# Attention with a threshold, then a Fourier mix and a two-layer network: row statistics behind the masking, a new order of early transfers and a fifth room for raw weights

## The chip, the core and the metric

The kernel runs on one core of one Trainium2 chip. The time is the device time of one execution in microseconds (us). The kernel before takes 1598.78 us, the median of three runs (1594.14 to 1601.38).

## What is computed

The inputs are q, k and v (8 batches, 8 heads, 576 rows, 64 columns, FP32), a scalar tau and two weight matrices that come in 64 bits (512 x 2048 and 2048 x 512).

```python
scores = q @ k.T / 8
scores = where(scores >= max(scores) - tau, scores, -1e9)      # per row
attn = softmax(scores);  x = attn @ v                          # heads side by side: 576 x 512
u = x + real(fft(fft(x, rows), columns))
un = (u - mean(u)) / sqrt(var(u) + 1e-6)                       # per row of 512
out = u + relu(un @ w_ch1) @ w_ch2
```

## The kernel before, in words

**Steps.** A batch has four pairs of heads, a pair five tiles of 128 query rows, so a batch is 20 steps and the kernel 160. A step computes scores of a tile for both heads (L434; L440 for the last, half tile), row maxima on VectorE (L455, in late steps L512), exponentials on ScalarE (L463, L518), and on VectorE the masking, which compares scores with the threshold, multiplies and sums (L471, L532). The scores stand in two PSUM tiles of two banks each, so the next step's scores wait for the masking. The tile of the step before is transposed on TensorE (L579 to L597) and copied to SBUF by ScalarE; at tiles 1 and 3 a product with v follows (L628).

**Everything is in an order written out by hand.** Each engine takes its instructions in program order, and so does SyncE, whose queue holds nearly all transfers. A transfer is asked for where its call stands in the program, and one that must wait for its room holds back all that are behind it.

**The first batch** (`step`) runs attention alone, filled up with small products (`busy`, L111). Beside it the first weight matrix comes in as 16 chunks of 512 KB. `staged` (L323) gives a chunk its room of raw 64-bit numbers in `hs`: four rooms, in turn. `convert` turns a chunk into FP32 in stages, one call of `next` each: the request (L283), two integer operations on VectorE (L293, L296), two on ScalarE (L301, L304), an add on VectorE (L308), a product on GpSimd (L313), a sign on ScalarE and another product on GpSimd (L315, L316). Step i takes the first stage of chunk i between its maxima and its masking, and the add and last stages of chunk i-1; its request for chunk i+3 comes near its end. Column means of the weights (L357) follow at step 6 and on. Ahead of step 0 stand the requests for the first chunks, for the two Fourier tables (`load_dim` L238 and L240, `load_seq` L215 and L217; L240 and L217 overwrite part of what the request before them brought, and wait for it) and for v; GpSimd copies the tables into their places (`copy_dim`, `copy_seq`, which ends by clearing the tile `f`, L228).

**The second batch** (`second_batch`, steps 20 to 39, numbered `first` = 0 to 19) also mixes batch 0 and begins the network on its rows, in portions that `fill` hands out. The 16 chunks of the second matrix are converted beside it. PLAN gives for each chunk the step of its first stage, the chunk, the room of its raw numbers and the step that asks for it: `h0` to `h3` are rooms in `hs`, a digit is a part of the second matrix's own tile that is not yet filled, `tmp` is a scratch tile. `transfers(first)` (L1634) asks for the chunks of a step, behind its masking.

**The late batches** run attention of one batch beside mix and network of the one before. Groups of 512 rows go through the network in a form with fewer products (`two_level`, L1179 and L1366). `Rows.load` (L837 to L847) transposes 128 rows of u, copies them with four ScalarE instructions (L842, L843) and takes their statistics on VectorE at once (L845, L846). A late step hands out network work three times: `fill(True)` between the exponentials and the masking (`softmax_second`), and two more behind it. `Rows.factors` (L852) takes the square root of the four tiles' variances on ScalarE, with two table loads (L853, L856), and a reciprocal on VectorE (L857). At a batch change the folds of the last pair (L679 to L695) and of the whole batch (L710 to L741) run on VectorE, and the first products of the mix (L751) wait for them.

Of the kernel before, what the change touches and what calls it, by code (L numbers as in the profile page):

```python
# [9 lines left out]
FP32 = mybir.dt.float32  # L10
# [37 lines left out]
def kernel(  # L48
# [12 lines left out]
    nc = tc.nc  # L61
# [12 lines left out]
    WC = 512  # L74
# [7 lines left out]
    sb = ctx.enter_context(tc.tile_pool(name="sb", bufs=2))  # L82
# [153 lines left out]
    def load_dim():  # L236
        raw = sb.tile([128, DM], FP32, tag="tmp", bufs=1, name="dim_raw")
        nc.sync.dma_start(out=raw[:, :], in_=dft_dim[0:128, :])  # L238

        nc.sync.dma_start(out=raw[0:1, EH:DM], in_=dft_dim[128:129, EH:DM])  # L240
        return raw
# [79 lines left out]
        return run  # L321

    def staged(n, src, dst):  # L323
        c0 = (0, 3 * WC, 6 * WC, 13 * WC)[n % 4]
        stage = hs[:, c0 : c0 + 3 * WC].bitcast(INT32).rearrange("p (c n) -> p c n", c=3)
        return chunk(src, dst, stage[:, 0:2, :], stage[:, 2, :])

    def w1_chunk(n):
        g, c = divmod(n, ND)
        cols = slice(WC * g, WC * (g + 1))  # L330
        return staged(n, w_ch1[128 * c : 128 * (c + 1), cols], w1[c][:, cols])
# [61 lines left out]
    def scale_q(n):  # L393

        raw = loaded[n][0]
        nc.scalar.activation(out=raw[:, :], in_=raw[:, :], func=ACT.Copy, scale=q_scale[:, :])
# [96 lines left out]
    def spread_inverse(i):  # L493
        e, den = steps[i]
        if i % NT == 4:
            nc.scalar.copy(e[:, S : S + 64], e[:, 512:S])
        if den is None:
            return
        nh = den.shape[1]
        rec = sb.tile([128, 2 * D], FP32, tag="rec", name="rec")  # L500
        nc.scalar.copy(
            rec[:, :].rearrange("p (j d) -> p j d", j=nh), _repeated(den, 2 * D // nh)
        )
        steps[i] = (e, rec)
# [309 lines left out]


    warm = const.tile([128, 1], FP32, name="warm")
    out_rows = out.rearrange("b s d -> (b s) d")

    COLS1, COLS2 = 28 * 4096, 49 * 2048
# [5 lines left out]
    class Rows:  # L825
# [7 lines left out]
        def load(self, t):  # L833
            c0 = (self.first + 128 * t) % RING
            pn = ps.tile([128, 512], FP32, tag="mm", bufs=4, name="pn")
            for c in range(ND):
                nc.tensor.transpose(  # L837
                    pn[:, 128 * c : 128 * (c + 1)], u_t[:, c, c0 : c0 + 128], ident[:, :]
                )
            u = sb.tile([128, DM], FP32, tag="u", bufs=4, name="u")  # L840
            for c in (0, 256):
                nc.scalar.copy(u[:, c : c + 129], pn[:, c : c + 129])  # L842
                nc.scalar.copy(u[:, c + 129 : c + 256], _reversed(pn[:, c + 129 : c + 256]))  # L843
            stats = sb.tile([128, nc.vector.BN_STATS_DIM], FP32, tag="stats", name="stats")
            nc.vector.bn_stats(stats[:, :], u[:, :])  # L845
            nc.vector.bn_aggr(self.mv[:, t, :], stats[:, :])  # L846
            self.us[t] = u  # L847

        def loaded(self):
            return all(u is not None for u in self.us)  # L850

        def factors(self):  # L852
            nc.scalar.activation(  # L853
                out=self.rstd[:, :], in_=self.mv[:, :, 1], func=ACT.Sqrt, bias=eps[:, :], scale=1.0
            )
            nc.scalar.activation(out=warm[:, :], in_=eps[:, :], func=ACT.Exp)  # L856
            nc.vector.reciprocal(self.rstd[:, :], self.rstd[:, :])  # L857
# [584 lines left out]
    late = []  # L1442
    ended = []
# [31 lines left out]
    def step(i):  # L1475

        n, t = divmod(i, NT)
        scores(i)

        def stages(count):  # L1480
            for _ in range(count if i - 1 in chunks else 0):
                next(chunks[i - 1], None)

        def next_stages():
            if i in chunks:
                next(chunks[i])
            stages(2)

        def last_stage():
            stages(1)  # L1490
            chunks.pop(i - 1, None)

        if t == 1 and n > 0:
            softmax(i, lambda: weighted_values(n - 1, 1), next_stages, last_stage)
            load_v(n + 1)
        elif t == 3:
            softmax(i, lambda: weighted_values(n, 0), next_stages, last_stage)
        else:
            softmax(i, None, next_stages, last_stage)
        if t == 1 and n > 0:  # L1500
            pass
        elif later and later[0][0] <= i:
            later.pop(0)[1](i)
        else:
            busy(2 if i < NCHUNK else 1)
        if t == 2:
            scale_q(n + 1)
        if t == 3:
            prep_pair(n + 1)
        if t == 1:  # L1510
            prep_ends(n)
        if i > 0:
            transposed_weights(i - 1)
        if i in chunks:
            next(chunks[i])
        while after and after[0][0] <= i:
            after.pop(0)[1]()
        if i > 0 and i + 3 < NCHUNK:
            chunks[i + 3] = w1_chunk(i + 3)
        if t == 2 and n > 0:  # L1520
            folds.append(fold_rows(n - 1))
        if folds and next(folds[0], True):
            folds.pop(0)
        spread_inverse(i)

    folds = []
    later = []
# [21 lines left out]
        means[g] = mean  # L1549

    chunks = {0: w1_chunk(0)}
    raw = load_dim()
    load_seq()
    chunks[1] = w1_chunk(1)
    scale_q(0)
    prep_pair(0)
    load_v(0)
    chunks[2] = w1_chunk(2)
    chunks[3] = w1_chunk(3)
    load_v(1)  # L1560
    copy_dim(raw)
    copy_seq()
    LAST = HID // WC - 1
    for g in range(LAST):
        center(g)
# [4 lines left out]
    while after:  # L1570
# [1 line left out]

    PLAN = (
        (1, 15, "h0", 0), (2, 14, "h1", 0), (3, 13, "h2", 0), (4, 12, "h3", 0),
        (5, 11, "0", 0), (5, 10, "1", 0), (6, 9, "2", 0), (7, 8, "h3", 5),
        (8, 7, "0", 6), (8, 6, "1", 6), (9, 5, "tmp", 4), (9, 4, "h3", 8),
        (10, 3, "0", 9), (11, 2, "h3", 10), (12, 0, "tmp", 10), (14, 1, "tmp", 13),
    )
    chunks = {}

# [4 lines left out]
    def transfers(first):  # L1585
        for at, j, room, issue in PLAN:
            if issue == first:
                chunks.setdefault(at, []).append(second_chunk(j, room))
# [30 lines left out]
    def second_batch(i):  # L1619

        nonlocal budget
        n, t = divmod(i, NT)
        first = i - per_batch
        if first != 1:
            scores(i)
        if first == 0:

            transposed_weights(i - 1)
        softmax(
            i, None, lambda: (advance(first), advance(first - 1), advance(first - 1)),  # L1630
            lambda: advance(first - 1),
        )
        chunks.pop(first - 1, None)
        transfers(first)  # L1634
        fold_more()
        if first == 0:
            weighted_values(n - 1, 1)
            scores(i + 1)
            column_means(LAST)
            copy_mean(LAST)  # L1640
            folds.append(fold_rows(n - 1))
            while folds:
                fold_more()
            load_v(n + 1)
            start_batch(0)
            mix(3)
            mix(3)
        elif first == 1:
            mix(3)
            transposed_weights(i - 1)  # L1650
            mix(2)
            mirrored(LAST)
            for c, eng in ((1, nc.vector), (3, nc.vector), (0, nc.gpsimd), (2, nc.gpsimd)):
                less_mean(eng, LAST, c)
            advance(first)
        elif first == 2:
            mix(2)
            transposed_weights(i - 1)
            mix(2)
            weighted_values(n, 0)  # L1660
            advance(first)
        else:
            fill()
            transposed_weights(i - 1)
            advance(first)
            fill()
            if t == 3:
                prep_pair(n + 1)
            fill()
            if t == 2:  # L1670
                weighted_values(n, 0)
            if t == 0:
                weighted_values(n - 1, 1)
                folds.append(fold_rows(n - 1))
                load_v(n + 1)
        if t == 1:
            prep_ends(n)
        if t == 2:
            scale_q(n + 1)
        if first == 16:  # L1680
            fold_halves(1)
        if first < 3:
            budget += 3 * per_slot
        spread_inverse(i)
# [8 lines left out]
    for i in range(2 * per_batch, total):  # L1693
# [20 lines left out]
        fill(True)  # L1714
        if i < total:
            softmax_second(i)
        while held:
            held.pop(0)()
        if mixes:
# [62 lines left out]
    for _ in range(3):  # L1782
        mix(1)
        fill(True)
        while held:
            held.pop(0)()
        if wanted:
            wanted.pop().factors()
    ended.append(True)
    per_slot = cost(0) / 40  # L1790
    while mixes or work:
# [47 lines left out]
```

## Time and profile before

| | |
|---|---|
| median of three runs | 1598.78 us |
| the profiled execution | 1596.7 us |
| its span, first to last instruction | 1594.9 us |
| mean granted TensorE clock | 0.990 |
| idle before scores (L434) for the masking (L471), first 330 us | 15.7 us, 11 times |
| idle of VectorE before L293 for a chunk's transfer, first 330 us | 12.3 us, 5 times |
| idle of VectorE before the statistics (L845) | 52.2 us, 28 of 36 times |
| SyncE's queue, waiting in L283 for rooms, first 330 us | 64.3 us |

A window row gives busy time and number of instructions of each engine in that stretch, then the granted TensorE clock (1.00 is full), the share of the transfer engines and the traffic. A timeline row gives start and length in us, the engine, the line, what is written and read, how often, and in brackets how long the engine stood idle before it and what ended that. PE is TensorE, PEld its weight loads, DVE VectorE, ACT ScalarE, POOL GpSimd, SPq SyncE's queue. A matrix product counts twice[...].

### The profile page before, as it was taken

Reading aid. Unit: us, or ns where it says so; the run is one execution under the profiler, and the core shown is the slowest. Engines: PE = TensorE matmul, PEld = TensorE weight load, DVE = VectorE, ACT = ScalarE, POOL = GpSimd, SP = SyncE. Lnnn points to the kernel's source line nnn. Section 1 sums busy time; section 2 is a strip of 40 time slices with the busy share of each in tenths; the row PEclk is TensorE's granted clock in tenths of the full one; section 3 lists DMA queues with packets and bytes.
Section 4 is the critical chain, followed back from the end, with each engine's and each line's share of the span. In section 5 each row is a group of like instructions: output and inputs, shape, how many; then the busy total and the mean of one; then the engine's idle time right before and its main releaser. Section 6 shows DMA issues by size and latency. Waiting matters only on the chain.

```text
span 1594.9 us, 27001 instructions
## 1 busy us (share of the span) xinstructions
PE 1538.0 (96%) x9786; PEld 1189.4 (75%) x9786; DVE 1060.9 (67%) x2119; ACT 918.6 (58%) x1921; POOL 775.2 (49%) x961
## 2 busy tenths in 40 slices
PE   7989989999999999989999999999999999999999
PEld 4555445555888777877787778877787778889999
DVE  6887766755868566775668466756567566655546
ACT  5875766554665666656666567656666676222231
POOL 5672554024445552646253643545264725546735
PEclk9999999999999999999999999999999999999999
DMA  5523221556956354634455344634464434646655
GB/s 149 132 67 115 75 77 37 152 156 206 292 174 198 93 159 128 202 97 146 131 167 162 105 147 129 208 87 146 128 192 129 144 120 157 211 140 234 234 193 185
DMA packets 248907, 239.31 MB, mean 150 GB/s; under 512 B 197027, under 2 KB 218533, under 8 KB 228678
## 3 DMA queue, kind: packets, MB, share of 16 engines
q1 hardware_dynamic: 246262, 237.28, 48.7%
q8 instruction: 78, 1.28, 0.3%
q10 hardware_dynamic: 2512, 0.30, 0.1%
q14 instruction: 55, 0.45, 0.1%
HBM read 205.93 MB, written 31.46 MB: 149 GB/s over the span
## 4 chain that ended last, share of the span: by engine, by line
PE 79%; DVE 12%; ACT 3%; issue 2%; DMA 2%; POOL 1%; SPq 1%; DVEq 0%; ACTq 0%; POOLq 0%
PE ph L1179 24%; PE po L1366 17%; PE pv L628 9%; PE sc L434 8%; PE pw L597 6%; PE po L902 4%; PE ph L878 2%; PE sc L440 2%; PE py L751 2%; PE pa L768 1%; PE pe L579 1%; PE pa L772 1%; PE po L1345 1%; ACT e L518 1%; DVE e L471 1%
## 5 line engine op out<-in xcount | busy, mean ns | idle before, releaser
L518 ACT ACTIVATE e<-sc,neg 128x576 f32<-128x576 f32 x216 | 158.6, 734 | 143.9 <-DVE neg L512 143.4
L512 DVE TENSOR_REDUCE neg<-sc 128x1 f32<-128x576 f32 x216 | 154.0, 750 | 116.7 <-PE sc L434 108.3
L1366 PE MATMUL po<-w,w_all 128*128 128x128 f32 x1728 | 220.1, 277 | 0.8 <-ACT ends L585 0.7
L1366 PEld LDWEIGHTS po<-w,w_all 128*128 128x128 f32 x1728 | 205.8, 192 | 10.3 <-issue 6.9
L1116 DVE TENSOR_TENSOR hs<-ph,hs 128x512 f32<-128x512 f32 (+1 forms) x128 | 105.3, 823 | 161.4 <-PE ph L1179 104.4
L1125 POOL TENSOR_TENSOR w<-hs 128x512 f32<-128x512 f32 x32 | 42.1, 1320 | 318.0 <-ACT hs L1121 244.3
L434 PE MATMUL sc<-kT,qT 64*128 64x288 f32 x1024 | 171.5, 433 | 15.8 <-DVE e L471 15.7
L597 PE MATMUL pw<-ident,e 128*128 128x128 f32 x1152 | 171.2, 276 | 13.8 <-ACT x_first L635 9.0
L1179 PE MATMUL ph<-u_t,w 128*128 128x256 f32 x768 | 180.5, 381 | 0.9 <-DMA w<-f 0.8
L532 DVE SCALAR_TENSOR_TENSOR e<-sc,thr,e 128x576 f32<-128x576 f32 x216 | 168.1, 811 | 17.9 <-ACT thr L522 17.9
L599 ACT COPY e_t<-pw 128x512 f32<-128x512 f32 x256 | 148.7, 595 | 45.9 <-PE pw L597 44.6
L541 ACT ACTIVATE e<-e,den 128x576 f32<-128x576 f32 x216 | 157.5, 775 | 11.3 <-DVE den L385 10.3
L597 PEld LDWEIGHTS pw<-ident,e 128*128 128x128 f32 x1152 | 135.7, 141 | 31.6 <-ACT x_first L635 10.1
L1179 PEld LDWEIGHTS ph<-u_t,w 128*128 128x128 f32 x768 | 141.2, 190 | 23.7 <-issue 3.8
L1179 PE MATMUL ph<-w_all,w 128*128 128x256 f32 x672 | 157.3, 382 | 1.1 <-DVE w_all L1101 1.0
L434 PEld LDWEIGHTS sc<-kT,qT 64*128 64x128 f32 x1024 | 94.9, 187 | 70.6 <-issue 33.8
L1179 PEld LDWEIGHTS ph<-w_all,w 128*128 128x128 f32 x672 | 123.3, 190 | 24.3 <-issue 4.9
L1121 ACT ACTIVATE hs<-hs 128x512 f32<-128x512 f32 (+1 forms) x96 | 74.0, 771 | 113.0 <-DVE hs L1116 112.3
L1231 POOL TENSOR_TENSOR w_all<-w_all 128x128 f32<-128x128 f32 (+2 forms) x160 | 117.9, 754 | 29.9 <-DVE w_all L1386 22.4
L1366 PE MATMUL po<-w,hs 128*128 128x128 f32 x912 | 120.3, 279 | 0.0
L1366 PEld LDWEIGHTS po<-w,hs 128*128 128x128 f32 x912 | 110.5, 193 | 9.5 <-issue 7.3
L793 POOL TENSOR_TENSOR u_t<-x,tmp 128x289 f32<-128x289 f32 (+1 forms) x45 | 33.9, 754 | 133.3 <-DVE tmp L788 133.3
(223 smaller groups left out, 2946.3 us busy)
## 6 DMA issues: line engine op xcount, KB each, us to landing
w<-f SPq DMA_DIRECT2D x150, 1024.0 KB, 4.9
hs<-in_moe_w_ch_dram SPq DMA_DIRECT2D x23, 512.0 KB, 4.6
q_in<-in_q_dram SPq DMA_DIRECT2D x128, 72.0 KB, 3.3
out_dram<-u SPq DMA_DIRECT2D x36, 256.0 KB, 2.2
k_in<-in_k_dram SPq DMA_DIRECT2D x124, 72.0 KB, 2.6
v_in<-in_v_dram SPq DMA_DIRECT2D x64, 128.0 KB, 5.1
f<-w SPq DMA_DIRECT2D x14, 512.0 KB, 3.9
f<-w SPq DMA_DIRECT2D x7, 1024.0 KB, 4.7
```

What stands on the lines that cost most here:

```text
L434: nc.tensor.matmul(sc[j][:, c, 0:HALF], qT[hp, 128 * t : 128 * t + 128], kT[hp, k0 + HALF * c : k0 + HALF * (c + 1)], start=True, stop=True,)
L512: nc.vector.tensor_reduce(out=neg[:, j : j + 1], in_=sc[j][:, :, 0:HALF], axis=AXIS_XY, op=ALU.max, negate=True,)
L518: nc.scalar.activation(out=ej, in_=sc[j][:, :, 0:HALF], func=ACT.Exp, bias=neg[:, j : j + 1], scale=1.0)
L532: nc.vector.scalar_tensor_tensor(out=ej, in0=sc[j][:, :, 0:HALF], scalar=thr[:, j : j + 1], in1=ej, op0=ALU.is_ge, op1=ALU.mult, accum_out ...
L541: nc.scalar.activation(out=e[:, S * j : S * (j + 1)], in_=e[:, S * j : S * (j + 1)], func=ACT.Copy, scale=den[:, j : j + 1],)
L597: nc.tensor.transpose(pw[:, c, :], e[:, c0 : c0 + 128], ident[:, :])
L599: nc.scalar.copy(e_t[:, 4 * j : 4 * j + 4, qs], pw[:, :, :])
L628: nc.tensor.matmul(pv[64 * j : 64 * j + 64, 0:m], vt[:, 2 * c + j, :], e_t[:, 4 * j + c, 0:m] if c < 4 else ends[:, 0, 0:m], start=(c == 0 ...
L1116: nc.vector.tensor_tensor(out=to, in0=bank, in1=to if other is None else other, op=ALU.add)
L1179: nc.tensor.matmul(bank[:, 256 * q : 256 * q + 256].rearrange("p (two n) -> p two n", two=2), left[:, 256 * c + 128 * q : 256 * c + 128 * ...
L1231: return lambda: eng.tensor_tensor(out=to, in0=to, in1=other, op=ALU.add)
L1366: nc.tensor.matmul(to, lefts[m][j][:, s], right_[:, 128 * s : 128 * (s + 1)], start=jn in (0, 4) and s == 0, stop=s == 3, skip_group_check ...
```

## The change

There are three parts.

1. At the start, chunks 1 and 2, the first v, the loads of pair 1 and chunk 3 are asked for ahead of the two tables. The tables' copies on GpSimd move from before step 0 to the ends of steps 3 and 4. Raw chunks get a fifth room in `hs`.
2. In the second batch the requests of a step stand at its head, ahead of its scores, except in `first` = 0; PLAN has new rooms, and later first stages or requests for some chunks.
3. In the late batches the statistics of a loaded tile are put in a list, which is worked off behind the masking (`measure`), or in `factors` if that comes first. In the second batch, and once attention has ended, they are still taken at once.

```diff
     def staged(n, src, dst):
-        c0 = (0, 3 * WC, 6 * WC, 13 * WC)[n % 4]
+        c0 = (0, 3 * WC, 6 * WC, 13 * WC, 9 * WC)[n % 5]
...
+    measures = []
+
+    def measure():
+        while measures:
+            measures.pop(0)()
...
-            stats = sb.tile([128, nc.vector.BN_STATS_DIM], FP32, tag="stats", name="stats")
-            nc.vector.bn_stats(stats[:, :], u[:, :])
-            nc.vector.bn_aggr(self.mv[:, t, :], stats[:, :])
             self.us[t] = u
+
+            def statistics():
+                stats = sb.tile([128, nc.vector.BN_STATS_DIM], FP32, tag="stats", name="stats")
+                nc.vector.bn_stats(stats[:, :], u[:, :])
+                nc.vector.bn_aggr(self.mv[:, t, :], stats[:, :])
+
+            measures.append(statistics)
+            if ended or not late:
+                measure()
...
         def factors(self):
+            measure()
...
         spread_inverse(i)
+        if i == 3:
+            copy_dim(raw)
+        if i == 4:
+            copy_seq()
...
     chunks = {0: w1_chunk(0)}
+    chunks[1] = w1_chunk(1)
+    chunks[2] = w1_chunk(2)
+    load_v(0)
+    scale_q(0)
+    prep_pair(0)
+    chunks[3] = w1_chunk(3)
     raw = load_dim()
     load_seq()
-    chunks[1] = w1_chunk(1)
-    scale_q(0)
-    prep_pair(0)
-    load_v(0)
-    chunks[2] = w1_chunk(2)
-    chunks[3] = w1_chunk(3)
     load_v(1)
-    copy_dim(raw)
-    copy_seq()
...
     PLAN = (
         (1, 15, "h0", 0), (2, 14, "h1", 0), (3, 13, "h2", 0), (4, 12, "h3", 0),
-        (5, 11, "0", 0), (5, 10, "1", 0), (6, 9, "2", 0), (7, 8, "h3", 5),
-        (8, 7, "0", 6), (8, 6, "1", 6), (9, 5, "tmp", 4), (9, 4, "h3", 8),
-        (10, 3, "0", 9), (11, 2, "h3", 10), (12, 0, "tmp", 10), (14, 1, "tmp", 13),
+        (5, 11, "0", 0), (5, 10, "1", 0), (6, 9, "2", 0), (7, 8, "h3", 6),
+        (8, 7, "tmp", 4), (8, 6, "0", 7), (9, 5, "1", 7), (10, 4, "h3", 9),
+        (11, 3, "tmp", 10), (11, 2, "0", 10), (13, 1, "h3", 12), (14, 0, "tmp", 13),
     )
...
         first = i - per_batch
+        if first > 0:
+            transfers(first)
...
         chunks.pop(first - 1, None)
-        transfers(first)
+        if first == 0:
+            transfers(first)
...
             softmax_second(i)
+        measure()
...
             wanted.pop().factors()
+    measure()
     ended.append(True)
```

## The prediction

> **What bounds the kernel now.** I read the page first, then the table of windows of 10 us, then every idle stretch of TensorE longer than 0.25 us in its timeline, and last, at each of these stretches, the timelines of VectorE (DVE), GpSimd (POOL), ScalarE (ACT) and SyncE's queue (SPq). The page:
>
> ```profile
> PE 1538.0 (96%) x9786; PEld 1189.4 (75%) x9786; DVE 1060.9 (67%) x2119; ACT 918.6 (58%) x1921; POOL 775.2 (49%) x961
> ...
> PE   7989989999999999989999999999999999999999
> ...
> PEclk9999999999999999999999999999999999999999
> ```
>
> TensorE is the bound: 57 us of the span of 1594.9 us are idle, and the lowest digits stand in slices 0, 2, 5 and 17, three of them before 240 us. A mean granted clock of 0.990 costs another 0.01 x 1595 = 16 us at most. No edit changes TensorE's work, so 57 + 16 = 73 us is all that there is. The windows say where it lies (columns: busy us and count of PE, PEld, DVE, ACT, POOL; clock; DMA share; GB/s):
>
> ```profile
> 20.00:30.00 10.00, 5.84 (x26) 3.22 (x28) 6.67 (x17) 6.32 (x13) 5.23 (x8) 1.00 0.86 234
> 30.00:40.00 10.00, 10.00 (x47) 5.79 (x48) 7.74 (x19) 5.14 (x11) 3.70 (x3) 0.83 0.22 65
> ...
> 200.00:210.00 10.00, 6.95 (x43) 4.44 (x40) 8.41 (x19) 6.10 (x13) 6.68 (x10) 1.00 0.06 6
> 210.00:220.00 10.00, 8.67 (x26) 4.22 (x26) 6.07 (x15) 9.66 (x23) 5.30 (x4) 0.75 0.58 131
> ```
>
> In 20:30 and 200:210 TensorE stands for 4.2 and 3.1 us, and the stretch behind each runs at a lower clock. The first 330 us hold about 30 us of the 57. TensorE's timeline there, with the idle before each row and its releaser:
>
> ```profile
> 21.27 1.97 PE L434 MATMUL sc<-kT,qT 64*128 64x288 f32 x8 [2.37 <-DVE e L471]
> 29.14 2.18 PE L434 MATMUL sc<-kT,qT 64*128 64x288 f32 x8 [2.90 <-DVE e L471]
> ...
> 206.62 1.21 PE L440 MATMUL sc<-kT,q_ends 128*128 128x288 f32 x4 [3.05 <-DVE e L471]
> ...
> 215.02 2.24 PE L434 MATMUL sc<-kT,qT 64*128 64x288 f32 x6 [0.80 <-DVE e L471]
> ```
>
> Scores of a step need the bank that the masking (L471) of the step before frees. VectorE runs in order, and ahead of the masking stand the integer steps of a weight chunk (L293, L296) and the add of the one before (L308). So a late chunk stops the masking:
>
> ```profile
> 26.99 0.43 DVE L293 TENSOR_SCALAR w<-hs 128x512 int32<-128x512 int32 x1 [2.76 <-DMA hs<-in_moe_w_ch_dram]
> ...
> 221.82 0.43 DVE L293 TENSOR_SCALAR w_all<-w_all 128x512 int32<-128x512 int32 x1 [3.77 <-DMA w_all<-in_moe_w_ch_dram]
> ...
> 232.20 0.43 DVE L293 TENSOR_SCALAR w_all<-hs 128x512 int32<-128x512 int32 x1 [1.99 <-DMA hs<-in_moe_w_ch_dram]
> ```
>
> **Part 1, the order at the start and the fifth room.** Step 1 begins at 13.95. Chunk 1 is issued at 13.84, behind the tables, whose second pieces wait for their first (SPq idle until 8.87 and until 13.56). Chunks 2 and 3 go at 22.71. In the change chunks 1 and 2 follow chunk 0 (issued at 3.81), at about 4.2 and 4.6, and land by about 11; then come v0, and q and k of pair 1 once the transposes of pair 0 are done (9.3), to about 13.5; then chunk 3, the tables (to about 22.6 with their two waits of about 4 and 2 us) and v1. Chunk 4 of step 1 thus goes at about 25, as now (26.11), into the empty fifth room, and chunk 5 right behind it, where now it waits for a conversion (5.39 us for the two). Step 4 wants chunk 4 at 33 or later.
>
> Step 1: the integer steps can follow the two maxima at 16.8, in place of 18.69; add and masking then end at 18.9 in place of 21.14, and scores of step 2 start at 19.0 in place of 21.27: 2.25 us. TensorE's transposes end at 18.9, so they are late next and nothing more is to be had. Step 2: its 2.76 us of waiting go; scores of step 3 start at 24.1 in place of 29.14. Step 3 now takes 8.76 us from scores to scores, with the value product at 3.38 us where other places show 1.95; at full clock TensorE's list is 1.94 + 2.3 + 1.85 + 1.3 = 7.4: 1.35 us. Together 6.4 us by step 4. From step 5 on no step of this batch waits for a chunk now, so nothing more comes.
>
> The table copies move on POOL to the ends of steps 3 and 4. They are 5.3 us (8.90 to 14.2) and 4.9 us (14.34 to 19.27, the clearing of f at 2.13 us among them). Chunk conversion queued behind them on POOL (2.6 us a step) runs late by up to about 5 us at step 5, and catches up by step 8, as POOL is half idle there. Who waits: the mean product of step 6 needs chunks 0 to 3, done at about 39, wanted at 47; the room of chunk 8 is needed at about 39; the copy ahead of the first row swap is late by 2 us, with its fold a step away. So I cost it at nothing, except by contention: POOL's clearing stood beside L293 at 0.85 us (0.43 elsewhere), and in 102:107 L296 and L308 took 1.70 and 1.95 (0.42 and 0.68) beside POOL's two-input ops. Bounds 0 and 5 us (two steps of 2.5); these are one-input copies, near the first row: 0.5 us.
>
> A rule of the Trainium skill speaks against this reordering: DMA: Bandwidth & Descriptors, section "Queues, rings and completion order", has the transfer engines take turns between queues by packets. k of pair 0 is in flight on ACT's queue (issued 1.18 to 3.95, wanted at 5.74) when the chunks start. By plain sharing, 1 MB more at the 138 GB/s of 0:10 would delay the start by up to 7 us. By the rule a longer SyncE queue takes no larger share than chunk 0 alone takes now, and the row has k landing at 5.74 beside chunk 0: 0. I take 0 and keep 2 us as the bad end. Part 1 is 5.9 us, from 0 to 6.4.
>
> **Part 2, requests at the head of a step and the new plan (second batch).** Chunk 8 moves from step 5 to the head of step 6, and on SyncE's queue that is behind a row swap and a v load: from 183.71 to about 192.9. It lands at about 197 and is wanted at 194.6, a new wait of 2 us in step 7. Masking there ends at 199.5 now, partly because POOL's fold slowed three ops from 1.5 to 3.5 us, and TensorE is busy until 201.1 with a value product: the wait hides; if that cover failed it would cost 2. Step 8 keeps its two chunks, so the stall of 3.05 us at 206.62 stays. Step 9 loses one of two chunks and its wait of 1.50: the masking moves from 214.15 to about 212, and the 0.80 us at 215.02 go. In step 10 the wait of 3.77 becomes one of about 2 (its chunk goes behind pair loads, 209.5 to 214.0), under TensorE's 3.6 us product: 0.80 us at 224.67 go. In step 11 the wait of 1.99 goes and with it 0.97 us at 234.45. The 1.94 us at step 14 opened no gap: 0. Sum 2.6 us. If the low clock of 210:230 goes too, another 3.4 (products 6.04 against 3.60, scores 2.24 against 1.21).
>
> On that clock: the skill's page TensorE: Matmul & The Clock Gate, "Part 1: The HAM clock gate", puts the halving after an idle window of about 3.4 us. The rows are harsher: a gap of 2.90 (29.14) was enough, and 215.02 followed 3.05 + 0.52 + 0.80. By the rule no gap of 3.05 alone should halve it, and the 3.4 us would all be won; by the rows the 3.05 remain and may do it. I take half, 1.7. Part 2 is 4.3 us, from 1 to 6.
>
> **Part 3, statistics behind the masking.** Statistics cost 0.69 + 0.18 us. In the late steps they stop VectorE 25 times for ScalarE's copies, 48.6 us, but TensorE hardly waits for it: its gaps lie at the batch changes.
>
> ```profile
> 1043.26 0.66 PE L597 MATMUL pw<-ident,e 128*128 128x128 f32 x4 [2.19 <-ACT x_first L635]
> ...
> 1384.33 0.49 PE L751 MATMUL py<-dim_c,f 128*128 128x128 f32 x2 [2.82 <-DVE f L732]
> ```
>
> Take 1022 to 1043. Now: statistics 1022.37 to 1023.2, after 3.16 us of waiting, masking to 1024.7, fold from 1025.03. Changed: masking 1019.2 to 1021, statistics to 1023.2, fold from 1023.3. But behind the fold's first four ops VectorE takes the reciprocal (L857), which waits for ScalarE's Sqrt (ends 1028.2), and ScalarE gets there only 0.35 us earlier. VectorE is then busy without a pause to 1043. So 0.35 us at each of five changes: 1.75 us.
>
> After the last attention step it turns round. The third and fourth statistics now lie ahead of the fold (1354.82, 1365.37); in the change both are queued at the factors, behind the fold's first four ops. The fold can start at 1365.75 (now 1366.31) as x comes then; four ops to 1369.2, two statistics to 1370.95, and Sqrt waits for them, so the reciprocal moves from 1369.64 to 1371.35. VectorE is busy from there to the stall at 1384.33, which grows by 1.7 us. Part 3 is 0; from -6 (the five gaps close) to +5 (the last one halves the clock, 3.4).
>
> **Sum.** 5.9 + 4.3 + 0 = 10.2 us. The profiled execution took 1596.7 us (span 1594.9 and 1.8 around it): 1586.5. Its time stands 2.1 below the median of 1598.8, so about 1589, 0.6% faster. What a measurement tells from no change is about 0.5%, 8 us: below 1590.8.
>
> **Rivals.**
> The likeliest, 0.5: as summed, 1583 to 1594.
> Gain mostly given back, 0.26: the copies on POOL slow VectorE by 3 us, the clock of 210:230 stays low, the end costs 1.7 + 1.7: 5.9 - 2.5 + 2.6 - 3.4 = 2.6, so 1596. For it speaks 102:107; against it, that the copies are short and have one input.
> Slower, 0.11: late statistics hold Sqrt at every batch change, not only the last. Where they stand behind the fold, ScalarE stops by 1.7 us and exponentials with it; the gaps of 2.19 to 2.62 us become 3.9 and more and pass the point where the clock halves (2.9 by the rows). Price: 5 x 1.7 + 5 x 3.4, less the 6.8 lost there now (0.91 in 680:720, 0.96 in 840:880 and 1040:1080), plus 5.1 at the end: 23.8, less 10.2: 1612. Against it: the fourth statistics stand before the fold in four of five changes.
> All gaps close, 0.13: 6.4 + 6.0, the 3.05 and most of the five gaps of 2.2 with their clock: 1577.
>
> Below 1590.8: 0.37 of the likeliest's 0.5, the 0.13 and 0.02 of the second, 0.52. Above 1606.8: 0.10. Between: 0.38. The range 1579 to 1599 leaves out the slower rival and half of the best.
>
> **What would show it.** Right: no wait for hs before chunk 1's and 2's L293, scores of step 4 at about 31.5 in place of 37.9, clock 1.00 in 30:40; in step 7 a new wait of 2 us without a gap on TensorE; the stall of 3.05 still there; gaps of about 1.9 at the batch changes; the last one at 4.5. Wrong: first scores later than 10.5 (k delayed), TensorE idle in steps 4 and 5, or a batch change whose reciprocal waits for Sqrt longer than now.

## The result, and the profile after

The changed kernel takes 1591.53 us, the median of 20 executions (1588.42 to 1594.62); the kernel before takes 1597.15 us, the median of 20 beside it (1593.69 to 1603.0). The ratio is 0.9961, with a 95% interval of 0.995 to 0.9972: 0.4% faster, where 0.6% was forecast. The median lies just above 1590.8, in the stretch to 1606.8 that I had given a chance of 0.38. The profiled execution took 1591.6 us, against 1596.7.

The page of the kernel after has these lines for those shown of before:

```profile
PE 1537.3 (97%) x9786; PEld 1189.8 (75%) x9786; DVE 1054.1 (66%) x2119; ACT 917.1 (58%) x1921; POOL 777.3 (49%) x961
...
PE   8989989999999999999999999999999999999999
```

The counts are equal, so no work has gone. The digits of slices 0 and 17 have risen, from 7 to 8 and from 8 to 9; those of slices 2 and 5 are as before. The windows of the kernel after:

```profile
20.00:30.00 10.00, 9.32 (x53) 5.14 (x51) 8.93 (x23) 9.68 (x21) 6.13 (x8) 1.00 0.40 105
30.00:40.00 10.00, 10.00 (x46) 6.15 (x45) 9.12 (x21) 7.92 (x20) 9.70 (x30) 1.00 0.71 167
40.00:50.00 10.00, 7.65 (x31) 4.17 (x31) 8.64 (x15) 5.82 (x13) 8.70 (x15) 0.66 0.42 151
...
210.00:220.00 10.00, 8.67 (x45) 4.76 (x45) 7.46 (x19) 9.22 (x24) 7.45 (x6) 1.00 0.80 204
```

In 20:30 TensorE is busy for 9.32 us in place of 5.84, as hoped. But 40:50, with 0.94 us of idle and a whole clock before, now has 2.35 us of idle and a clock of 0.66. In 210:220 the clock is 1.00 in place of 0.75. TensorE's timeline:

```profile
10.91 1.24 PE L434 MATMUL sc<-kT,qT 64*128 64x288 f32 x8 [1.88 <-DVE qT L408]
...
20.40 1.97 PE L434 MATMUL sc<-kT,qT 64*128 64x288 f32 x8 [0.28 <-DVE e L471]
25.77 1.97 PE L434 MATMUL sc<-kT,qT 64*128 64x288 f32 x8 [0.39 <-DVE e L471]
32.89 1.14 PE L440 MATMUL sc<-kT,q_ends 128*128 128x288 f32 x4
36.76 1.50 PE L434 MATMUL sc<-kT,qT 64*128 64x288 f32 x8
43.18 3.00 PE L434 MATMUL sc<-kT,qT 64*128 64x288 f32 x8 [2.35 <-DVE e L471]
52.12 1.45 PE L434 MATMUL sc<-kT,qT 64*128 64x288 f32 x8
...
205.23 1.21 PE L440 MATMUL sc<-kT,q_ends 128*128 128x288 f32 x4 [3.06 <-DVE e L471]
```

The gaps of 2.37 and 2.90 us are now 0.28 and 0.39, and scores of step 4 start at 32.89 in place of 37.90. The new gap of 2.35 stands at the head of step 6, and scores of step 7 start at 52.12, where they started at 52.58 before: of 5 us of lead 0.5 are left. The gap of 3.05 us in the second batch is as it was. VectorE's waits for a chunk in the second batch, and the two kinds of gap of the late stages:

```profile
195.43 0.68 DVE L293 TENSOR_SCALAR w_all<-hs 128x512 int32<-128x512 int32 x1 [1.98 <-DMA hs<-in_moe_w_ch_dram]
...
216.29 0.43 DVE L293 TENSOR_SCALAR w_all<-hs 128x512 int32<-128x512 int32 x1 [1.51 <-DMA hs<-in_moe_w_ch_dram]
```

```profile
1038.70 0.66 PE L597 MATMUL pw<-ident,e 128*128 128x128 f32 x4 [2.19 <-ACT x_first L635]
...
1379.44 0.49 PE L751 MATMUL py<-dim_c,f 128*128 128x128 f32 x2 [2.99 <-DVE f L732]
```

The new wait of 2 us for chunk 8 is there (1.98). The gap at a batch change is 2.19 as before, and that at the last one 2.99 in place of 2.82.

**Where the time went.** VectorE adds up each step's denominators right behind the masking (L382), once a step. The lead of a kernel is the start of that instruction in the trace of before, less its start in the kernel's own trace. One row for each profile, in us, positive where it is ahead of before:

| kernel | step 0 | 4 | 5 | 7 | 26 | 35 | 45 | 80 | 85 | 155 |
|---|---|---|---|---|---|---|---|---|---|---|
| after | -1.2 | 4.9 | 3.5 | 0.5 | 1.3 | 5.9 | 4.3 | 3.1 | 4.5 | 5.1 |
| part 1 alone | -1.0 | 5.1 | 4.0 | 1.8 | 1.0 | 1.6 | 1.1 | 0.2 | 0.2 | -1.7 |
| part 2 alone | -0.2 | 0.2 | 0.1 | 0.1 | -0.1 | 4.5 | 2.8 | 2.9 | 2.9 | 3.2 |
| part 3 alone | -0.4 | -0.3 | -0.3 | -0.3 | -0.5 | -0.6 | -1.1 | -2.1 | 0.8 | 0.9 |
| copies alone | -0.5 | 0.5 | 0.3 | -1.8 | -2.6 | -2.6 | -3.0 | -3.2 | -3.2 | -3.3 |
| copies in pieces | -0.6 | 5.8 | 5.6 | 3.9 | 4.3 | 8.6 | 8.6 | 8.7 | 11.1 | 11.6 |
| the same, without part 3 | -1.2 | 5.2 | 5.0 | 3.3 | 3.7 | 7.8 | 7.8 | 5.2 | 6.2 | 5.2 |

In the kernel after, part 1 leaves 0.5 us by step 7. From step 26 to 35, the second batch, 4.6 us are won. From 35 to 80 2.8 us are lost again, 1.6 of them by the clock (0.83 in 280:290, where it was 1.00), in rows of the attention and the network that the change leaves as they are; between 80 and 85 1.4 us come. My theory after this look: what part 1 wins is eaten in steps 5 and 6 by GpSimd's late work, and part 2 carries the result. The rival: the parts are worth what was forecast, and single traces mislead by the clock.

### The profile page after: what moved, and what is told of

It reads as the page before. It is cut to its first block, busy times and chain, and to the rows that moved or that the text cites. A ratio compares the mean times of both kernels' runs of the same rounds, so it can differ in the third digit from the quotient of the medians.

```text
span 1589.8 us, 27001 instructions
## 1 busy us (share of the span) xinstructions
PE 1537.3 (97%) x9786; PEld 1189.8 (75%) x9786; DVE 1054.1 (66%) x2119; ACT 917.1 (58%) x1921; POOL 777.3 (49%) x961
## 4 chain that ended last, share of the span: by engine, by line
PE 81%; DVE 10%; ACT 5%; issue 1%; DMA 1%; POOL 0%; SPq 0%; DVEq 0%; ACTq 0%
PE ph L1192 24%; PE po L1379 17%; PE pv L628 10%; PE sc L434 9%; PE pw L597 7%; PE po L915 4%; PE ph L891 2%; PE sc L440 2%; PE py L751 2%; PE pa L768 1%; DVE neg L455 1%; PE pa L772 1%; PE pe L579 1%; ACT e L518 1%; DVE e L471 1%
```

## The experiments

Times are medians; a ratio is to the kernel before on the same chip, with its 95% interval. A kernel of this section was executed 6 to 12 times.

**One part at a time.** Kernel before with part 1 alone (the new order, the fifth room, `copy_dim` and `copy_seq` behind steps 3 and 4):

> Kernel before with part 1 alone: new order of the transfers at the start, fifth room, table copies behind steps 3 and 4. My theory: what the new order gains in steps 1 to 3 (5.0 us of lead by step 4) is lost again in step 5 (VectorE's integer steps run beside GpSimd's late multiplications, a gap of 2.35 us, a halved clock), so that 0.5 us are left at step 7 and the whole is 0.5 to 1.3 us faster than before (about 1596). Rival, the forecast as it stood: 5.9 us faster (about 1591). If part 1 is worth over 4 us alone, the loss in step 5 belongs to the parts together.

1598.69 us, ratio 1.0012 (1.0 to 1.0025). Part 1 wins nothing; the forecast of 5.9 us falls, and so does my theory's 0.5 to 1.3. The lead is 5.1 at step 4 and 1.8 at step 7, and goes on falling to -1.7 by step 155, in steps that part 1 does not touch.

Kernel before with part 2 alone (`transfers(first)` at the head, the new PLAN):

> Kernel before with part 2 alone: requests at the head of a step and the new plan of the second batch. My theory: nearly all of the change's gain is here, 4.3 to 5 us faster than before (about 1592.3), with the clock of 210:230 at 1.00 and the gap of 3.05 us at the next-to-first of its stalls still there. Rival: the clock in 210:230 stays low without part 1's time shift, and only the 2.6 us of gaps are won (about 1594.5).

1593.18 us, ratio 0.9978 (0.9964 to 0.9991): 3.5 us. Its windows, and the stall that stays:

```profile
210.00:220.00 10.00, 8.66 (x39) 4.57 (x39) 7.66 (x19) 9.28 (x24) 6.21 (x5) 1.00 0.78 184
220.00:230.00 10.00, 10.00 (x54) 5.48 (x52) 7.16 (x20) 5.76 (x13) 4.14 (x4) 1.00 0.21 63
```

```profile
206.65 1.21 PE L440 MATMUL sc<-kT,q_ends 128*128 128x288 f32 x4 [3.09 <-DVE e L471]
```

The clock stays whole behind a stall of 3.09, and the lead rises by 4.6 us. That is my theory's number in the trace, and a little less in the medians.

Kernel before with part 3 alone (`measure`):

> Kernel before with part 3 alone: the row statistics behind the maskings. My theory: nothing, within 1 us of before (about 1597). Rivals: it gains 2 us or more by itself (the waits of the masking for ScalarE's copies did cost something), or it loses 1.7 us and more at the last change, as I had forecast for that place.

1596.05 us, ratio 0.9982 (0.9967 to 0.9998). By the ratio it gains 2.9 us, so my "nothing" looks wrong, but the interval reaches to 0.3, and the medians (1597.19 for before) lie only 1.1 apart. What is shown are gaps. Two ahead of the second batch change, 0.73 and 0.84 us in before (at 680.66 and 689.63), are one of 0.30 here:

```profile
682.84 2.05 PE L1379 MATMUL po<-w,w_all 128*128 128x128 f32 x16 [0.30 <-ACT ends L585]
693.90 0.44 PE L579 MATMUL pe<-ident,e 128*128 128x128 f32 x1 [2.62 <-DVE w_all L1399]
```

They are 0.30 and none in the kernel after too, and 0.73 and 0.83 us with part 1 alone, 0.74 and 0.84 with part 2 alone, so it is part 3 that shortens them. That is 1.3 us; the other 1.6 of the lead that it gains between steps 80 and 85 is clock (680:700 at 0.91 in place of 0.83). The three ratios multiply to 0.9972, against 0.9961 for the whole: within their intervals the parts add up.

**The copies.** Kernel before with the table copies alone moved:

```diff
-    copy_dim(raw)
-    copy_seq()
...
         spread_inverse(i)
+        if i == 3:
+            copy_dim(raw)
+        if i == 4:
+            copy_seq()
```

> Kernel before with the table copies alone moved behind steps 3 and 4; the order of the transfers is the old one. My theory: GpSimd's multiplications of chunks 4 to 6 are pushed back and run beside VectorE's integer steps of the next chunk, as in the changed kernel; one or two of these steps take 1.2 to 1.8 us in place of 0.42 and the maskings of steps 5 and 6 are late by 1 to 2.5 us: 1 to 2.5 us slower than before, so that the order itself is worth 1 to 2.5 us more than part 1 as a whole. Rival: the old order leaves room, 0.

1600.84 us, ratio 1.0027 (1.0014 to 1.004): 4.3 us slower, more than expected; in the trace 2.1 us of lead go between steps 5 and 7. Beside part 1 alone (1.9 us slower) the new order of the transfers would be worth about 2.4 us of time, not the 5.1 us of lead at step 4, but the two intervals overlap. GpSimd's rows and VectorE's of this kernel, where it happens, and TensorE's wait for it:

```profile
47.07 2.12 POOL L228 MEMSET f<- 128x2432 f32 x1
49.27 1.48 POOL L313 TENSOR_TENSOR w<-w,hs 128x512 f32<-128x512 f32 x1
50.84 1.35 POOL L316 TENSOR_TENSOR w<-w,hs 128x512 f32<-128x512 f32 x1
```

```profile
49.20 0.42 DVE L293 TENSOR_SCALAR w<-hs 128x512 int32<-128x512 int32 x1
49.53 1.50 DVE L296 TENSOR_SCALAR hs<-hs 128x512 int32<-128x512 int32 x1
50.96 1.78 DVE L308 SCALAR_TENSOR_TENSOR w<-hs,w 128x512 f32<-128x512 uint32 x1
```

```profile
53.62 0.72 PE L434 MATMUL sc<-kT,qT 64*128 64x288 f32 x2 [1.26 <-DVE e L471]
```

The clearing of `f` ends at 49.19, and only then the multiplications of step 5 begin, which stand at 45.88 and 47.23 in before, while VectorE masks and then waits for scores. Here the first, 49.27 to 50.75, meets L296, which begins at 49.53 and ends at 51.03; the second, to 52.19, meets L308, which ends at 52.74. VectorE's two instructions end 0.28 and 0.55 us behind GpSimd's, a little less than their own lengths of 0.42 and 0.68. In before, at 102:107, L296 and L308 end 0.29 and 0.55 us behind the GpSimd operations beside them. So the integer step ends some 0.28 us and the add 0.55 us behind GpSimd in both kernels: this looks like waiting, not like running slower. The Trainium skill says so (SBUF — State Buffer, "SBUF: two separate sides"): VectorE and GpSimd share a pair of ports that one holds for its whole instruction while the other stands, if VectorE's reads through two ports or has two inputs. These rows agree with it; that L293 and L296, with one input each, read through two ports is not shown by a trace.

In the kernel after the same happens a step earlier. GpSimd's and VectorE's rows there:

```profile
38.99 1.29 POOL L316 TENSOR_TENSOR w<-w,hs 128x512 f32<-128x512 f32 x1
40.22 0.36 POOL L220 MEMSET seq_xe<- 128x290 f32 x1
40.49 0.35 POOL L221 MEMSET seq_xo<- 128x288 f32 x1
...
46.10 1.27 POOL L313 TENSOR_TENSOR w<-w,hs 128x512 f32<-128x512 f32 x1
47.45 1.36 POOL L316 TENSOR_TENSOR w<-w,hs 128x512 f32<-128x512 f32 x1
```

```profile
39.38 1.75 DVE L293 TENSOR_SCALAR w<-hs 128x512 int32<-128x512 int32 x1
41.05 0.53 DVE L296 TENSOR_SCALAR hs<-hs 128x512 int32<-128x512 int32 x1
...
47.58 1.52 DVE L296 TENSOR_SCALAR hs<-hs 128x512 int32<-128x512 int32 x1
```

L293 ends 0.85 us behind L316, and 0.29 us behind the second of the two short clearings that follow it (L221, to 40.84), as if held by all three. It loses 1.33 us, so the masking ends late, and with it come the scores of step 6 at 43.18. At 47.58 L296 meets L316 once more and ends 0.29 us behind it.

**The copies in pieces.** The changed kernel, with every copy and clearing of the two tables its own entry of a list (`f` cleared in four), of which four are worked off behind each step; line numbers stand 4 higher in it:

```diff
-        if i == 3:
-            copy_dim(raw)
-        if i == 4:
-            copy_seq()
+        for _ in range(4):
+            if tables and i > 2:
+                tables.pop(0)()
```

> The changed kernel with the table copies on GpSimd cut into single operations, four behind each step from step 3 on (the clearing of the fold's buffer in four), in place of all of one table behind step 3 and all of the other behind step 4. My theory: the copies delay GpSimd's multiplications of a chunk by 4 us so that they run beside VectorE's integer steps of the next one (1.75 us in place of 0.43); spread, the multiplications end in time, the gap of 2.35 us at the head of step 6 falls to about 1, the clock of 40:50 stays at 1.00, and the kernel is 3 to 4 us faster than the changed one (about 1588). Rival: the chain of maskings in step 5 is long by itself, the gap stays over 2 us and the clock low; then nothing is won (1591.5).

1586.53 us, ratio 0.994 (0.992 to 0.9959): 5.0 us below the changed kernel by the medians, 3.4 by the ratios, whose intervals overlap by a little. GpSimd's multiplications of step 4 and TensorE's scores of step 6:

```profile
35.42 1.29 POOL L317 TENSOR_TENSOR w<-w,hs 128x512 f32<-128x512 f32 x1 [2.35 <-DVE w L312]
36.78 1.29 POOL L320 TENSOR_TENSOR w<-w,hs 128x512 f32<-128x512 f32 x1
```

```profile
41.05 1.94 PE L438 MATMUL sc<-kT,qT 64*128 64x288 f32 x8 [1.19 <-DVE e L475]
42.92 4.06 PE L632 MATMUL pv<-e_t,v_rev 128*64 128x320 f32 x16
```

The multiplications start 2.2 us earlier than in the kernel after and are over when VectorE's integer step comes (38.55); the gap is 1.19 in place of 2.35, as expected, and L297 takes 0.56 us where L293 took 1.75. The clock of 40:50 isn't 1.00 but 0.83, yet the lead at step 7 is 3.9 in place of 0.5. Not all of the 5 us are from here: against the kernel after this one is 3.4 us ahead at step 7, 2.7 at step 35 and 5.6 at step 80; the last 2.9 are the clock's (in the kernel after 0.83 in 280:290 and 0.98 in 500:600, here 1.00 in both). Nor are all meetings gone: 1.7 us of lead still go between steps 5 and 7.

The same kernel without part 3:

> The kernel with the tables' copies in single operations (which took 1586.5 us, a ratio of 0.9940 to before), with the row statistics again ahead of the masking, as in the kernel before. My theory: part 3 is worth its own run's 0.2% or less, so this one takes 1586.5 to 1589. Rival: part 3 is worth nothing or costs at the last change, so this one is as fast or faster (1585 to 1586.5).

1590.95 us, ratio 0.995 (0.9933 to 0.9968). It lies above the expected range of 1586.5 to 1589, on the side of a gain by part 3; its gap of 0.84 is back (684.43).

**Is it the gap, or VectorE?** The changed kernel with `busy(4)` in place of `busy(2)` in step 5:

```diff
-            busy(2 if i < NCHUNK else 1)
+            busy(4 if i == 5 else 2 if i < NCHUNK else 1)
```

> The changed kernel with four filler products in place of two behind the scores of step 5 (1.7 us of work on TensorE more, whose results nobody reads). They stand in the gap of 2.35 us at the head of step 6 and lengthen nothing else. My theory: the gap is then 0.6 us, the clock of 40:50 stays at 1.00, and the 3 us that the low clock cost there (scores 3.00 in place of 1.94, value product 4.78 in place of 2.31) are won: 2.5 to 3.5 us faster than the changed kernel (about 1588.5), while VectorE's integer steps stay slow (1.75 us). Rival: the low clock was no cost, since VectorE is late in steps 6 and 7 too; then the time is as the changed kernel's, 1591.5, or up to 1.7 longer.

1593.06 us, ratio 0.9962 (0.9947 to 0.9977), the same as the changed kernel's. TensorE's rows in it:

```profile
43.05 1.97 PE L434 MATMUL sc<-kT,qT 64*128 64x288 f32 x8 [0.24 <-DVE e L471]
44.95 2.37 PE L628 MATMUL pv<-e_t,v_rev 128*64 128x320 f32 x16
...
50.55 0.72 PE L434 MATMUL sc<-kT,qT 64*128 64x288 f32 x2 [1.45 <-DVE e L471]
```

The gap is filled, the clock of 40:50 is 1.00 and the value product takes 2.37 us (4.31 in the kernel after). And all the same of a lead of 3.5 at step 5 only 1.3 are left at step 7: now step 7's scores wait 1.45 us, because the masking of step 6 is late as well. My theory that the low clock cost 3 us there falls, and the rival holds: VectorE, held by GpSimd, sets the pace in both steps, and the low clock lay for the most part in time that TensorE would have waited.

With the copies in pieces, one more filler product in step 5 (`busy(3 if i == 5 ...)`):

> The kernel with the tables' copies in single operations, and three filler products in place of two in step 5 (0.86 us of work more, in a gap of 1.19 us). In that kernel step 6 lost 1.7 us to a value product of 4.06 us at a halved clock, in the one without part 3 the same product took 2.37 us. My theory: which of the two happens is decided by the clock alone, and with a gap of 0.3 us the clock of 40:50 is 1.00: the lead of 5.6 us at step 5 is kept, 0.7 to 1.7 us faster (about 1585.5). Rival: VectorE is late by as much in step 6 (as with the filler in the changed kernel), then 0 to 0.3 us.

1589.93 us, ratio 0.9948 (0.9931 to 0.9965): no gain to be seen. The value product takes 2.37 us, and of a lead of 6.2 us at step 5 there are 4.5 left at step 7: 1.7 us go, as many as without the filler product (5.6 to 3.9). The rival holds again.

**The late start.** In the profile of before, the first transpose waits for k of pair 0 until 7.45, in that of after until 9.01. Here is the row of before, then that of after:

```profile
7.45 0.78 DVE L405 STREAM_TRANSPOSE kT<-k_in 128x576 f32<-128x576 f32 x1 [3.30 <-DMA k_in<-in_k_dram]
...
9.01 0.78 DVE L405 STREAM_TRANSPOSE kT<-k_in 128x576 f32<-128x576 f32 x1 [4.85 <-DMA k_in<-in_k_dram]
```

The changed kernel with chunk 2 and the first v behind the loads of pair 1:

```diff
-    chunks[2] = w1_chunk(2)
-    load_v(0)
     scale_q(0)
     prep_pair(0)
+    chunks[2] = w1_chunk(2)
+    load_v(0)
```

> The changed kernel with only chunks 0 and 1 requested ahead of pair 0's preparation; chunk 2 and the first v load go behind the loads of pair 1. My theory: k of pair 0 lands late (VectorE's first transpose at 9.01 in place of 7.45 us) because more bytes ask at once; with 0.85 MB less ahead of it the transpose starts at 7.5 to 8.3 and the first scores near 9.9 in place of 10.91, about 1 us earlier; chunk 2, wanted at 23.4, still lands in time. Of that 1 us some is lost to the gap of step 5, which stays: 0 to 1 us faster than the changed kernel (about 1591). Rival: the transpose stays at 9.0, since the start waits for something else than shared transfer engines.

1594.51 us, ratio 0.9976 (0.9962 to 0.9991); the transpose starts at 8.83, and nothing is won. And the kernel with the copies in pieces, with `raw = load_dim()` right behind chunk 0, ahead of chunk 1:

> The kernel with the tables' copies in single operations, and the cosine table of the columns requested right behind chunk 0 (as before the change): its second piece waits for its first, to about 8.9 us, and so holds chunks 1 and 2 back until k of pair 0 has landed. My theory: chunk 1's request at 4.3 us, right behind chunk 0's, is what delays k; so the first transpose of k stands at 7.5 us again (8.4 to 9.0 with chunk 1 ahead, 8.83 also without chunk 2 and v0), first scores at about 9.7, and 0.6 to 0.9 us are won that last, as chunks 1 and 2 still land by 13 and 17 us (wanted at 17.5 and 22.5): about 1586.0. Rival: the table itself takes the place of chunk 1 and k stays late, 0.

1589.29 us, ratio 0.9947 (0.993 to 0.9964); the transpose starts at 8.26. Both expectations of the cause fail. The start scatters by itself: with chunk 0 and the table ahead, the first scores start at 9.56 (before), 9.82 (part 2), 9.92 (part 3) and 10.22 (copies alone), with chunk 1 right behind chunk 0 at 9.68 to 10.92 in eight profiles, 10.50 on the mean against 9.88. This kernel and the last one below, which both ask for the table behind chunk 0, lie at 10.16 and 9.67. So 0.6 us of the 1.35 seen first may be due to the order; the rest is within the scatter.

**Another plan.** The changed kernel with one chunk less at step 8:

```diff
-        (8, 7, "tmp", 4), (8, 6, "0", 7), (9, 5, "1", 7), (10, 4, "h3", 9),
-        (11, 3, "tmp", 10), (11, 2, "0", 10), (13, 1, "h3", 12), (14, 0, "tmp", 13),
+        (8, 7, "tmp", 4), (9, 6, "0", 7), (10, 5, "1", 7), (11, 4, "h3", 9),
+        (11, 3, "tmp", 10), (12, 2, "0", 11), (14, 1, "h3", 13), (14, 0, "tmp", 13),
```

In this plan rooms are taken again too early for part of the second matrix, whose values are then not the reference's; the instructions and their order are as written.

> The changed kernel with another plan in the second batch: step 8 converts one chunk in place of two (chunk 6 moves to step 9, 5 to 10, 4 to 11 beside 3, 2 to 12, 1 and 0 to 14). My theory: the gap of 3.06 us at 205.23 is the two chunks' integer steps and add ahead of the masking (2.36 us on VectorE for both); with one chunk 0.8 us fewer stand there, and the gap falls to about 2.2: 0.8 to 1 us faster (about 1590.6), unless step 14 with two chunks opens a gap of its own of as much. Rival 1: the gap vanishes (3 us faster), as TensorE's work of step 9 can go ahead. Rival 2: nothing, because step 8's masking waits for ScalarE or for its scores.

1590.62 us, ratio 0.9951 (0.9936 to 0.9966), not to be told from the changed kernel's 0.9961. The gap:

```profile
204.03 2.26 PE L440 MATMUL sc<-kT,q_ends 128*128 128x288 f32 x4 [2.42 <-DVE e L471]
```

It shrinks by 0.64 us, near the 0.8 of my theory, but by step 35 the lead gained since step 26 is 4.0 us, less than the 4.6 of the kernel after; what took its place was not followed up.

**The best order that the runs point to.** The table asked for behind chunk 0, its copies at once where GpSimd is idle (9 to 15 us), the other table's in pieces behind steps 3 to 6:

```diff
     chunks = {0: w1_chunk(0)}
+    raw = load_dim()
...
     scale_q(0)
     prep_pair(0)
+    copy_dim(raw)
+    while tables:
+        tables.pop(0)()
```

> As the kernel with the cosine table requested behind chunk 0 and all copies in single operations (1589.3 us, ratio 0.9947), but the copies of that table run at once, from about 9 to 15 us, where GpSimd has nothing else to do; only the other table's 14 operations stay behind steps 3 to 6. My theory: what is lost in steps 5 to 7 (a lead of 5.7 us at step 5, 4.0 at step 7) comes from those 14 operations and stays; the 26 that go cost 0.2 us in steps 7 to 14. So 0.2 us, not to be told from 1589.3; the ratio to before is 0.994 to 0.9955. Rival: GpSimd's copies of steps 7 to 12 delay multiplications that collide later too (1.65 us for an integer step at 49.9), then up to 1.5 us faster, near 1588.

1588.69 us, ratio 0.9948 (0.9934 to 0.9962), as the theory said. The four kernels with copies in pieces and part 3 lie at 0.994 to 0.9948, all below the kernel after's 0.9961. The interval of each overlaps that of the kernel after (0.995 to 0.9972), so the gain over it, 2 to 3 us, rests on the four together; that they differ among each other is not shown.

## Why the prediction was right, and where it wasn't

**The total** was 10.2 us and is 5.6 by the medians. The direction, the range and the second batch held; part 1 didn't. That the total came as near as this is in part luck: part 1, forecast at 5.9 us, brought nothing, and part 3, put at nothing, brought about 3 us by gaps that I had not looked at.

**Part 1, steps 1 to 3: right.** 6.4 us were forecast by step 4. The lead goes from -1.2 at step 0 to 4.9 at step 4, which is 6.1 won; the waits for chunks 1 and 2 are gone, and the clock of 30:40 is 1.00.

**Part 1, the copies: the step that failed.** "So I cost it at nothing, except by contention ... one-input copies, near the first row: 0.5 us." The run with the copies alone is 4.3 us slower. I had seen that the chunk's conversion on GpSimd would run late by up to 5 us, and asked who waits for its result: nobody does. I did not ask beside what it would then run. The price came from the two-input multiplications that the copies pushed onto VectorE's integer steps, at 1.1 to 1.3 us for each meeting, and the rows at 102:107, which I had quoted and set aside, showed that price. VectorE has little slack there (8.50 us busy of 10 in 40:50 of before), so each meeting moves the masking. My bad end of 5 us was nearer. Part 1 alone (from 0 to 4 us slower) lies below the 0 that I had as the low end of its range. Of the signs of being wrong that I had named, scores later than 10.5 (10.91) and an idle TensorE ahead of step 6 (2.35 us) were both there.

**Part 1, the start: 0 taken, 2 kept as the bad end.** 1.35 us were seen, some 0.6 on the mean of the profiles. My "k landing at 5.74" was a wrong reading: that is a row of ScalarE, and VectorE's transpose waits for k until 7.45 in before too. The rule of the Trainium skill that I weighed there (DMA: Bandwidth & Descriptors, "Queues, rings and completion order": the transfer engines take turns between queues by packets) let me expect that a longer queue takes nothing from k. The profiles lean against that by 0.6 us, but with a scatter of over 1 us between kernels of nearly the same start they do not settle it.

**Part 2: the sum right, its terms not.** 4.3 us were forecast, and 4.6 of lead (3.5 in the medians of part 2 alone) came. But the gaps gave next to nothing. Before, those from 211 to 239 are 0.52, 0.80, 0.80, 0.97 and 1.16, in sum 4.25. In the kernel after:

```profile
211.50 0.66 PE L597 MATMUL pw<-ident,e 128*128 128x128 f32 x4 [0.54 <-ACT u L849]
218.41 2.38 PE L628 MATMUL pv<-e_t,v_rev 128*64 128x320 f32 x16 [0.79 <-ACT e_t L601]
230.50 0.33 PE L582 MATMUL pe<-ident,rec 128*128 128x128 f32 x1 [1.52 <-ACT rec L501]
233.32 3.70 PE L891 MATMUL ph<-u_t,w 128*128 128x512 f32 x8 [1.19 <-ACT ends L585]
```

They sum to 4.04, so 0.2 of my 2.6. The gap of 0.80 behind ScalarE's e_t, which I had down as gone, is still there, and one of 1.52 behind ScalarE is new: once VectorE no longer waits for chunks, ScalarE is late next. What came is the clock: the products at 6.04 and scores at 2.24 us of before are 3.70 and 1.24, 3.3 us together. With the gaps' 0.2 this makes 3.5 of the 4.6 us of lead; the rest I have not placed. Of the clock's share I had taken half. The profiles say that half is about right as a mean: of the nine with the new plan five are at full clock in 200:220, but in three the clock of 200:210 is 0.66, behind a like stall (3.08 here):

```profile
200.00:210.00 10.00, 7.45 (x16) 4.25 (x17) 9.60 (x25) 7.57 (x19) 5.58 (x6) 0.66 0.29 47
```

That is the kernel with the table behind chunk 0; from step 26 to 35 it gains 2.6 us, not 4.6. The wait for chunk 8 (2 us forecast, 1.98 seen) opens no gap, and the 3.05 us stay, as said.

**Part 3: 0 forecast, about 3 measured (0.3 to 5.3).** At the batch changes the reciprocal waits for the square root. The rows of the statistics before, and of statistics and reciprocal after:

```profile
1022.37 0.69 DVE L845 BATCH_NORM_STATS2 stats<-u 128x6 f32<-128x512 f32 x1 [3.16 <-ACT u L843]
...
1018.02 0.69 DVE L854 BATCH_NORM_STATS2 stats<-u 128x6 f32<-128x512 f32 x1 [1.04 <-ACT u L849]
...
1023.45 0.18 DVE L870 RECIPROCAL rstd<-rstd 128x4 f32<-128x4 f32 x1 [2.33 <-ACT rstd L866]
```

VectorE's waits for ScalarE ahead of the statistics fell from 52.2 to 20.7 us in all, but here the wait has for the most part only moved: 3.16 us ahead of the statistics became 1.04 there and 2.33 ahead of the reciprocal. At all five changes the reciprocal now waits 2.3 to 3.1 us, where it waited 1.2 at the first and not at all at the others. That was a sign of being wrong in my list, but it misled: the square root is not later (from 1027.90 it moved to 1023.12, while the gap at the change moved from 1043.26 to 1038.70), VectorE only comes to it sooner. TensorE's gaps stay: the small gain of 0.35 at each change did not come (2.19 at 1038.70), nor the loss of 1.7 at the last (0.17). What I had not looked at are the gaps of 0.73 and 0.84 us ahead of the second change, of which part 3 leaves 0.30.

**The rivals.** "Gain mostly given back" had the right mechanism for part 1, GpSimd against VectorE, with 3 us; the rest of it (a low clock at 210:230, a worse end) did not come. "Slower" did not happen: the square root came no later, and no gap at a batch change grew but the last, by 0.17 us.

## What to carry to other kernels

When work is moved on one engine, ask not only who waits for what is queued behind it, but beside which instructions of other engines that will then run: on GpSimd and VectorE a delay by one operation turns into the length of a whole operation where they meet. Move many small operations as small portions, not as a block. (To let part of them fall into time in which the engine has nothing else to do brought no further gain that these runs can tell: 0.9948 against 0.9947.) And before a clock loss is counted as a gain to be had, see whether another engine would have held TensorE in that time anyway, as a filler product that cures the clock shows at once.

## What was not expected of the hardware

**The clock goes with the spread.** Over 29 executions of the kernel before on one chip (1590.9 to 1603.95 us), time and mean granted clock go together with a correlation of -0.86, at about 1.4 us for each 0.001 of clock; on the three other chips it is -0.87 to -0.94, at 0.9 to 1.1 us. So a kernel's single profile is uncertain by some 3 us. Part 1's 12 executions had a mean clock of 0.9877 against 0.9890, which by that slope makes 1.8 us, about that kernel's whole distance to before; whether part 1's own gaps lowered it is not shown.

Not all of such a difference need be chance. The kernel after lost 2.8 us of lead between steps 35 and 80, the one with copies in pieces, with the same program there, none. Behind one and the same gap of 1.41 us, between 281 and 286 us, the clock of 280:290 is 0.83 to 0.88 in all five profiles with a new plan and the copies as blocks, and 1.00 in all five with the copies in pieces. Some of the gain of the pieces may be this. Why the two groups differ was not found.

**Like gaps, unlike clocks.** Behind a gap of 1.19 us at the head of step 6 the value product took 4.06 us (copies in pieces), behind 1.17 us in the kernel with the table asked for first 2.37:

```profile
40.91 1.94 PE L438 MATMUL sc<-kT,qT 64*128 64x288 f32 x8 [1.17 <-DVE e L475]
42.78 2.37 PE L632 MATMUL pv<-e_t,v_rev 128*64 128x320 f32 x16
```

The Trainium skill's page TensorE: Matmul & The Clock Gate, "Part 1: The HAM clock gate", has a window of about 3.4 us that runs freely, and a kernel's phase in it left to chance; the differing outcomes agree with chance of that kind. That a gap of 1.2 us, a third of such a window, was followed by half clock at all does not agree with a wholly idle window being needed. What decides it was not found.
